# Two-MLP attention kernel: other PSUM banks for a pair's h, x forms of MLP 2 built during MLP 1's state rows, own buffers for the last evictions

## The chip, the cores and the metric

The kernel runs on one core of a Trainium2 chip. The metric is the device time of one execution in microseconds (us), the median of several. Work is spread over TensorE (PE; its weight loads are listed as PEld), VectorE (DVE), ScalarE (ACT) and the DMA queue that SyncE (SP) issues. Each engine runs its own list of instructions in order and waits on semaphores for the others.

## The reference

For 8 batch entries of 8 heads, 512 tokens and 32 states (D = 64), tokens attend to states and states attend to tokens; both results are laid side by side, so that there are 4608 rows of 512 numbers. Two MLPs with 2048 hidden units follow, the first with a squared ReLU, the second with an ELU:

```python
xread = softmax(scale * x @ state.T) @ state
sread = softmax(scale * state @ x.T) @ x
x = concat([xread, sread])              # rows of 512 = 8 heads x 64
x = relu(x @ w_in) ** 2 @ w_out         # MLP 1
h = x @ w_in2
out = where(h > 0, h, exp(min(h, 0)) - 1) @ w_out2   # MLP 2
```

## The kernel before, in words

Every product is made of three matmuls on operands that were split into a high part (an ACT copy) and a low part (a DVE subtraction); the helper `split` (L162) issues the two. Products of two token blocks at once use a seven-product scheme for 2x2 blocks, so they need sums of blocks ("forms") of x, of g and of the weights.

The work comes in this order. Batch entries 0 to 5 go one by one through MLP 1 (`block`, L477). Entries 6 and 7 go together (`pair`, L619): 32 tiles h (attention folded into m, `s1_x`), each read by a ReLU on ACT (L630), then `out_products` (L47) with its phases 1, 2, 6, 5, 7, 4, 3 of 48 matmuls into the accumulators x, y, z. Then come the 256 state rows of MLP 1 (L687 to L719): in turn i, PE makes h of slice i and adds slice i-2 to the four accumulators `acc`; ACT and DVE make the ReLU, its square, the split of that (gs) and the split of the next but one weight slice (`split_w1`, L449). Results of MLP 1 go through DRAM (`x2d`). MLP 2 reads them back (`load_xr`, L758), builds seven split forms of two entries (`x_forms`, L762: seven splits and four sums of 128x1024) and runs `first_product` and `second_product` for four such pairs, and last `state_block` (L884).

A scheduler orders each engine's list by its own model of time; pools decide which buffer or bank a tile gets. In the stage of the pair, PSUM has two banks for m (aux), and pools x, y, z of two banks in this order, which lie where `block` had its accumulators acc 0 and 1, acc 2 and 3, and its two h banks. The pair's h alternates between y and x (L624). In the state rows h lies on x, and acc on y and z; the weights v1 of the state rows (`load_v1`, L682) go into the 16 buffers gq1. MLP 2's own pools (L725 to L735) are opened after all of MLP 1's are closed. The last four evictions (L926) share three buffers `oo`.

Of the kernel before, what the change touches and what calls it, by code (L numbers as in the profile page):

```python
# [9 lines left out]
F32 = mybir.dt.float32  # L10
F32R = mybir.dt.float32r
# [3 lines left out]
ALU = mybir.AluOpType  # L15
AX = mybir.AxisListType

B, H, S, NS, D = 8, 8, 512, 32, 64
# [86 lines left out]
def attn_mlp_kernel(ctx: ExitStack, tc: tile.TileContext, xt, xn, st, w1, v1, w2, v2, outx, outs):  # L105
# [63 lines left out]
    if True:  # L169
# [270 lines left out]
        def operand_s():  # L440
            t = xc_p.tile([P, 2, KC, NST], F32R, name="sts", tag="xc")
            for k in range(2):
                split(t[:, HI, 2 * k:2 * k + 2], t[:, LO, 2 * k:2 * k + 2], stf[:, 2 * k:2 * k + 2])
            return t
# [163 lines left out]
        eu1_p = pool("eu1", 2)  # L608
        u21_p = pool("u21", 2)
        oo1_p = pool("oo1", 2)  # L610
        ps_x, ps_y, ps_z = [pool(n, 2, space=bass.MemoryType.PSUM) for n in ("psx1", "psy1", "psz1")]
        def weight1(j, f):
            t = wr1_p.tile([P, 2, 256], F32R, name="wr", tag="wr")
            src = {1: lambda: v1d[j][:, :, :256], 2: lambda: v1d[j + HF][:, :, :256],
# [4 lines left out]
        def pair(b0, bg):  # L619

            g = {q: [] for q in (11, 12, 21, 22)}
            for s in range(2 * FC):
                b, f = b0 + s // FC, s % FC
                ps = (ps_y, ps_x)[f % 2].tile([P, S], F32, name="h1", tag="yx"[f % 2])  # L624
                s1_x(b, ops[b], f, ps)
                t = g[(11, 12, 21, 22)[s // HF]]
                if f % 2 == 0:
                    t.append(gq1_p.tile([P, 2, S], F32, name="g1", tag="gq"))
                h = t[-1][:, f % 2]
                pace[:] = [nc.scalar.activation(out=h, in_=ps, func=AF.Relu)]  # L630
                if f % 2:
                    nc.vector.tensor_tensor(out=h, in0=h, in1=h, op=ALU.mult)
                else:
                    nc.scalar.activation(out=h, in_=h, func=AF.Square)
                if s >= 3 * HF and f % 2:
                    u = g[21][(f - HF) // 2]
                    nc.vector.tensor_tensor(out=u, in0=u, in1=t[-1], op=ALU.add)
                for todo in bg.get(s, ()):
                    todo()

            def step(n):
                for todo in bg.get(2 * FC + n, ()):
                    todo()

            def put(e, k, o):
                nc.sync.dma_start(out=x2d[b0 + e][:, k], in_=o)

            out_products(nc, split, g, weight1, 1, step, put, (gp1_p, eu1_p, u21_p, oo1_p), (ps_x, ps_y, ps_z))
# [28 lines left out]
            pair(b, bg)  # L677


        v1s = {}  # L680

        def load_v1(f):  # L682
            if f < FC:
                v1s[f] = gq1_p.tile([P, 2, DM], F32R, name="v1s", tag="gq")
                nc.sync.dma_start(out=v1s[f].bitcast(F32), in_=v1d[f])

        for f in range(4):  # L687
            load_v1(f)
        op = operand_s()
        gs = {}  # L690
        for i in range(FC + LAG):
            if i < FC:
                ps = ps_x.tile([P, NST], F32, name="h", tag="x")
                s1_s(op, i, ps)
                r = eu1_p.tile([P, NST], F32, name="r", tag="eu")
                nc.scalar.activation(out=r, in_=ps, func=AF.Relu)
                g = u21_p.tile([P, NST], F32, name="g", tag="u2")
                nc.vector.tensor_tensor(out=g, in0=r, in1=r, op=ALU.mult)
                t = gs[i] = gp1_p.tile([P, 2, NST], F32R, name="gs", tag="gp")
                split(t[:, HI], t[:, LO], g)  # L700
                if i + 2 < FC:
                    split_w1(i + 2)
                load_v1(i + 4)
            f = i - LAG
            if f < 0:
                continue
            if f == 0:
                acc = [p.tile([P, NST], F32, name="acc", tag=c) for p, c in ((ps_y, "y"), (ps_z, "z")) for _ in range(2)]
            w, t = v1s.pop(f), gs.pop(f)
            for k in range(KC):  # L710
                sl = slice(k * P, (k + 1) * P)
                mm3(acc[k], (w[:, HI, sl], w[:, LO, sl]), (t[:, HI], t[:, LO]), f == 0, f == FC - 1)
        for k in range(KC):
            o = oo1_p.tile([P, NST], F32, name="o", tag="o")
            if k % 2:
# [1 line left out]
            else:  # L717
                nc.scalar.activation(out=o, in_=acc[k], func=AF.Copy)
            nc.sync.dma_start(out=x2d[B][:, k], in_=o)  # L719
        double.close()  # L720
        one.close()


    pool2 = lambda name, bufs, **kw: ctx.enter_context(tc.tile_pool(name=name, bufs=bufs, reuse_waits="tile", **kw))
    xr_p = pool2("xr", 2)  # L725
    xf_p = pool2("xf", NF)
    wr_p = pool2("wr", 12)
    eu_p = pool2("eu", 5)
    u2_p = pool2("u2", 2)
    gq_p = pool2("gq", FC)  # L730
    gp_p = pool2("gp", 3)
    oo_p = pool2("oo", 3)
    ps_y = pool2("psy", 2, space=bass.MemoryType.PSUM)
    ps_z = pool2("psz", 3, space=bass.MemoryType.PSUM)
    ps_x = pool2("psx", 3, space=bass.MemoryType.PSUM)  # L735
    act, tt = nc.scalar.activation, nc.vector.tensor_tensor
    DM1, DM2 = slice(0, 2), slice(2, 4)

    def elu(h, out):

# [10 lines left out]
    def weight(name, j, f):  # L751
        t = wr_p.tile([P, 2, 256], F32R, name="wr", tag="wr")
        nc.sync.dma_start(out=t.bitcast(F32), in_=wf[name, j][:, f - 1])
        return t

    xf, xr = {}, {}

    def load_xr(b):  # L758
        xr[b] = xr_p.tile([P, KC, S], F32, name=f"xr{b}", tag="xr")
        nc.sync.dma_start(out=xr[b], in_=x2d[b])  # L760

    def x_forms(n):  # L762

        t1, t2 = xr[2 * n], xr[2 * n + 1]
        a11, a12, a21, a22 = t1[:, DM1], t1[:, DM2], t2[:, DM1], t2[:, DM2]

        def put(f, src):
            t = xf[n, f] = xf_p.tile([P, 2, 2, S], F32R, name=f"xf{n}_{f}", tag="xf")
            split(t[:, HI], t[:, LO], src)

        put(1, a11)
        yield
        put(2, a12)
        yield
        tt(out=a21, in0=a21, in1=a22, op=ALU.add)
        put(5, a21)
        yield
        tt(out=a11, in0=a21, in1=a11, op=ALU.subtract)
        put(6, a11)
        yield  # L780
        tt(out=a21, in0=a22, in1=a11, op=ALU.subtract)
        put(7, a21)
        yield
        put(4, a22)
        yield
        tt(out=a12, in0=a12, in1=a11, op=ALU.subtract)
        put(3, a12)
        yield

    def first_product(n, g):  # L790

# [92 lines left out]
    def state_block(prepared):  # L884
        for _ in prepared:
            pass
        nxt = iter(order[4:])
        ahead = iter(order[6:])

        def refill():  # L890
            x = next(nxt, None)
            if x:
                split_plain(*x)
            x = next(ahead, None)
            if x:
                load_plain(*x)

        gs, acc = {}, []
        for i in range(HF + 2):
            if i < HF:  # L900
                w = plain.pop(("w2", i))
                ps = ps_x.tile([P, 2, NST], F32, name="hs", tag="x")
                for r in range(2):
                    for d in range(2):
                        sl = [slice(r * 256 + k * P, r * 256 + (k + 1) * P) for k in range(2)]
                        product(nc, ps[:, r], [(w[:, HI, d, x], w[:, LO, d, x]) for x in sl],
                                [(xs[0][:, HI, 2 * d + k], xs[0][:, LO, 2 * d + k]) for k in range(2)],
                                r == 1 and d == 1, r == 0 and d == 0)
                g = gq_p.tile([P, 2, NST], F32, name="gsf", tag="gq")
                elu(ps, g)  # L910
                t = gs[i] = gq_p.tile([P, 2, 2, NST], F32R, name="gss", tag="gq")
                split(t[:, HI], t[:, LO], g)
                refill()
            j = i - 2
            if j < 0:
                continue
            if j == 0:
                acc = [p.tile([P, NST], F32, name="as", tag=c) for p, c in ((ps_y, "y"), (ps_z, "z")) for _ in range(2)]
            w, t = plain.pop(("v2", j)), gs.pop(j)
            for r in range(2):  # L920
                for m in range(KC):
                    sl = slice(m * P, (m + 1) * P)
                    product(nc, acc[m], [(w[:, HI, r, sl], w[:, LO, r, sl])], [(t[:, HI, r], t[:, LO, r])],
                            j == HF - 1 and r == 1, j == 0 and r == 0)
            refill()
        for m in range(KC):  # L926
            o = oo_p.tile([P, NST], F32, name="o", tag="o")
            if m % 2:
                nc.vector.tensor_copy(out=o, in_=acc[m])
            else:  # L930
                act(out=o, in_=acc[m], func=AF.Copy)
            nc.sync.dma_start(out=outs[m * P:(m + 1) * P, :], in_=o)

    for b in range(2):
        load_xr(b)
    for _ in x_forms(0):
        pass
    for n in range(B // 2):
        g = {}
# [51 lines left out]
```

## Time and profile before

| what | value |
|---|---|
| median of 3 runs | 1353.41 us (1352.47 to 1356.91) |
| span of the profiled execution, first to last instruction | 1350.5 us |
| its whole device time | not given by the page |
| PE busy | 1327.5 us, 98% of the span |
| PEld, DVE, ACT busy | 78%, 70%, 62% |
| granted TensorE clock, mean | 0.997 of full speed |

Busy shares are averages over the whole span. Where PE stands still is read from the list of waits and from the order of time; "idle before" in a row is the time in which the engine stood before that instruction, with what ended it.

### The profile page before, as it was taken

The page shows a single profiled execution, that of the slowest core. Times are in us where ns is not written, and L with a number is a line of the kernel's source. Part 1 is how long each engine was busy: PE and PEld are TensorE (multiplying, and loading weights), DVE is VectorE, ACT ScalarE, POOL GpSimd, SP SyncE. Part 2 cuts the span into 40 slices and gives each one's busy share as a digit, 9 for nine tenths or more (in the row PEclk, how much of TensorE's full clock was granted, in tenths as well). Part 3 has the DMA queues.
Part 4 walks back from the last instruction along what each step waited for, and adds up shares of the span by engine and source line. Part 5 has one row for each costly group of instructions (what it writes and reads, how often), then busy time and mean ns, then how long its engine had stood idle before and what let it go on. Part 6 is the DMA issues. An engine that isn't in the chain of part 4 may idle for free.

```text
span 1350.5 us, 19746 instructions
## 1 busy us (share of the span) xinstructions
PE 1327.5 (98%) x7064; PEld 1057.1 (78%) x7064; DVE 951.0 (70%) x1437; ACT 839.5 (62%) x1417; POOL 0.7 (0%) x6
## 2 busy tenths in 40 slices
PE   8989999999999999999999999999999999999998
PEld 6656777777777776778988888888888888888898
DVE  6997868686878865775576884579636884568644
ACT  5887758676777657644467843676446743666444
POOL 0000000000000000000000000000000000000000
PEclk9999999999999999999999999999999999999999
DMA  6988856575857424279077777767776777778732
GB/s 240 318 300 310 305 178 230 201 267 190 279 197 266 151 82 153 97 255 349 25 252 208 224 240 224 208 194 247 229 225 194 206 210 223 209 204 284 226 110 100
DMA packets 127729, 290.72 MB, mean 215 GB/s; under 512 B 13840, under 2 KB 22032, under 8 KB 124560
## 3 DMA queue, kind: packets, MB, share of 16 engines
q1 hardware_dynamic: 127632, 289.46, 66.3%
q8 instruction: 56, 0.92, 0.3%
q14 instruction: 41, 0.34, 0.1%
HBM read 212.86 MB, written 76.55 MB: 214 GB/s over the span
## 4 chain that ended last, share of the span: by engine, by line
PE 89%; DMA 5%; DVE 3%; ACT 3%; issue 1%; SPq 0%; ACTq 0%; DVEq 0%
PE x L43 16%; PE X L43 13%; PE z L43 8%; PE Z L43 6%; PE acc L158 6%; PE acc L159 6%; PE acc L160 6%; PE h L158 5%; PE h L159 4%; PE h L160 4%; PE y L43 4%; PE Y L43 3%; DMA raw_v<-in_v_dram 2%; PE mp L331 2%; PE hs L43 2%; PE as L43 2%
## 5 line engine op out<-in xcount | busy, mean ns | idle before, releaser
L163 ACT ACTIVATE gp<-g 128x1024 fp32r<-128x1024 f32 (+1 forms) x168 | 154.0, 917 | 146.0 <-PE x L43 69.5
L164 DVE TENSOR_TENSOR gp<-g,gp 128x1024 fp32r<-128x1024 f32 (+1 forms) x168 | 174.9, 1045 | 95.4 <-ACT gp L163 94.4
L43 PE MATMUL x<-gp,wr 128*128 128x512 f32 x960 | 223.5, 390 | 0.0
L43 PEld LDWEIGHTS x<-gp,wr 128*128 128x128 f32 x960 | 179.7, 188 | 39.4 <-ACT eu L71 1.9
L43 PE MATMUL X<-xf,wr 128*128 128x512 f32 x768 | 186.7, 390 | 0.0
L43 PEld LDWEIGHTS X<-xf,wr 128*128 128x128 f32 x768 | 143.4, 188 | 31.7 <-ACT u L748 1.3
L158 PE MATMUL acc<-gs,v 128*128 128x512 f32 x384 | 154.4, 402 | 3.8 <-DVE gs L474 1.9
L159 PE MATMUL acc<-gs,v 128*128 128x512 f32 x384 | 150.4, 392 | 0.0
L160 PE MATMUL acc<-gs,v 128*128 128x512 f32 x384 | 150.2, 392 | 0.0
L43 PE MATMUL z<-gp,wr 128*128 128x512 f32 x480 | 110.4, 389 | 0.0
L744 DVE SCALAR_TENSOR_TENSOR g<-r,g 128x512 f32<-128x512 f32 x96 | 63.9, 689 | 65.8 <-ACT r L743 65.8
L43 PEld LDWEIGHTS z<-gp,wr 128*128 128x128 f32 x480 | 90.1, 188 | 18.7
L158 PE MATMUL h<-at,m 128*128 128x512 f32 x256 | 103.0, 403 | 1.7 <-ACT r L469 1.7
L158 PEld LDWEIGHTS acc<-gs,v 128*128 128x128 f32 x384 | 72.0, 188 | 38.1 <-issue 15.9
L160 PE MATMUL h<-at,m 128*128 128x512 f32 x256 | 100.7, 395 | 0.5 <-ACT m L346 0.5
L159 PE MATMUL h<-at,m 128*128 128x512 f32 x256 | 101.0, 395 | 0.0
L43 PE MATMUL Z<-xf,wr 128*128 128x512 f32 x384 | 97.4, 389 | 0.0
L469 ACT ACTIVATE r<-h 128x512 f32<-128x512 f32 x96 | 57.1, 595 | 64.4 <-PE h L160 64.1
L742 ACT ACTIVATE r<-g 128x512 f32<-128x512 f32 x96 | 57.5, 625 | 57.5 <-DVE g L821 40.4
L160 PEld LDWEIGHTS acc<-gs,v 128*128 128x128 f32 x384 | 72.1, 188 | 19.8 <-issue 4.2
L159 PEld LDWEIGHTS acc<-gs,v 128*128 128x128 f32 x384 | 72.2, 188 | 18.6 <-issue 3.4
L43 PEld LDWEIGHTS Z<-xf,wr 128*128 128x128 f32 x384 | 72.1, 188 | 15.0
(145 smaller groups left out, 2173.6 us busy)
## 6 DMA issues: line engine op xcount, KB each, us to landing
wr<-f_v SPq DMA_DIRECT2D x256, 256.0 KB, 3.0
wr<-f_w SPq DMA_DIRECT2D x224, 256.0 KB, 2.9
f_v<-wf SPq DMA_DIRECT2D x40, 512.0 KB, 3.3
raw_w<-in_w_dram SPq DMA_DIRECT2D x32, 512.0 KB, 4.8
raw_v<-in_v_dram SPq DMA_DIRECT2D x32, 512.0 KB, 5.0
f_w<-wf SPq DMA_DIRECT2D x24, 512.0 KB, 2.8
xt<-in_xt_dram SPq DMA_DIRECT2D x8, 1024.0 KB, 6.9
xn<-in_xn_dram SPq DMA_DIRECT2D x8, 1024.0 KB, 6.1
```

Source lines behind the costliest of these rows:

```text
L43: nc.tensor.matmul(ps, wk[a], xk[b], start=start and k == 0 and i == 0, stop=last and k == len(w) - 1 and i == 2, skip_group_check=True)
L158: mm(ps, w[HI], x[LO], start=first, stop=False)
L159: mm(ps, w[HI], x[HI], start=False, stop=False)
L160: mm(ps, w[LO], x[HI], start=False, stop=last)
L163: copy = nc.scalar.activation(out=hi, in_=src, func=AF.Copy)
L164: nc.vector.tensor_tensor(out=lo, in0=src, in1=hi.bitcast(F32), op=ALU.subtract)
L331: mm(ps[e][32 * k:32 * k + 32, :], st_t[b][r, k, :], x(k, r), start=True, stop=True)
L469: pace[:] = [nc.scalar.activation(out=r, in_=ps, func=AF.Relu)]
L742: act(out=r, in_=h, func=AF.Relu, scale=-1.0)
L744: nc.vector.scalar_tensor_tensor(out=out, in0=r, scalar=-1.0, in1=h, op0=ALU.add, op1=ALU.max)
```

## The change

It does four things. The pools of the pair's stage are opened in the order y, x, z, and h alternates between z and y; h thus begins on `block`'s h banks and goes on with acc 0 and 1, and x is untouched until phase 1. The state rows get pools of their own (opened and closed again), and the buffers xr, wr and xf of MLP 2 are opened on SBUF's right side before the state rows; the weights v1 of the state rows use those wr buffers, in two halves, and the x forms of MLP 2's first pair are built in every second turn of the state rows. The last turn of `state_block` goes accumulator by accumulator, and its evictions use the five buffers eu.

```diff
-        ps_x, ps_y, ps_z = [pool(n, 2, space=bass.MemoryType.PSUM) for n in ("psx1", "psy1", "psz1")]
+        ps_y, ps_x, ps_z = [pool(n, 2, space=bass.MemoryType.PSUM) for n in ("psy1", "psx1", "psz1")]
...
-                ps = (ps_y, ps_x)[f % 2].tile([P, S], F32, name="h1", tag="yx"[f % 2])
+                ps = (ps_z, ps_y)[f % 2].tile([P, S], F32, name="h1", tag="zy"[f % 2])
...
+        double.close()
+        right = lambda name, bufs: ctx.enter_context(tc.tile_pool(name=name, bufs=bufs, side="right", reuse_waits="tile"))
+        xr_p = right("xr", 2)
+        wr_p = right("wr", 12)
+        xf_p = right("xf", NF)
+        rows = one.enter_context(ExitStack())
+        pool = pools(rows)
...
+        ps_y, ps_x, ps_z = [pool(n, 2, space=bass.MemoryType.PSUM) for n in ("psy2", "psx2", "psz2")]
...
         def load_v1(f):
             if f < FC:
-                v1s[f] = gq1_p.tile([P, 2, DM], F32R, name="v1s", tag="gq")
-                nc.sync.dma_start(out=v1s[f].bitcast(F32), in_=v1d[f])
+                v1s[f] = [wr_p.tile([P, 2, 256], F32R, name="v1s", tag="wr") for _ in range(2)]
+                for c, t in enumerate(v1s[f]):
+                    nc.sync.dma_start(out=t.bitcast(F32), in_=v1d[f][:, :, c * 256:(c + 1) * 256])
         for f in range(4):
             load_v1(f)
         op = operand_s()
+        for b in range(2):
+            load_xr(b)
+        forms = x_forms(0)
...
                 load_v1(i + 4)
+            if i > 1 and i % 2 == 0:
+                next(forms, None)
...
-            for r in range(2):
-                for m in range(KC):
+            last = j == HF - 1
+            for i in range(2 * KC):
+                r, m = (i % 2, i // 2) if last else divmod(i, KC)
...
-            o = oo_p.tile([P, NST], F32, name="o", tag="o")
+            o = eu_p.tile([P, NST], F32, name="o", tag="eu")
```

How the lists of instructions move, at the three places that the prediction speaks of. First PE's list from the last matmuls of entry 5 (acc) to the pair's first h (mp6_1 and mp6_2 are the products that become the next two slices of m). Before:

```order
L160 MATMUL acc_4501<-gs_5131,v1_15_1169 128x512
L331 MATMUL mp6_1_0_5272<-w1_10_322,st6_3872 32x512 [waits PE_49]
...
L331 MATMUL mp6_2_0_5326<-w1_20_489,st6_3872 32x512 [waits DVE_49]
L331 MATMUL mp6_2_1_5327<-w1_20_489,st6_3872 32x512 [waits DVE_49]
...
L158 MATMUL h1_5253<-at6_4710,m6_00_5017 128x512 [waits Activation_49]
```

and now:

```order
L160 MATMUL acc_4501<-gs_5131,v1_15_1169 128x512
L158 MATMUL h1_5253<-at6_4710,m6_00_5017 128x512
...
L331 MATMUL mp6_1_0_5272<-w1_10_322,st6_3872 32x512 [waits PE_49]
...
L158 MATMUL h1_5288<-at6_4710,m6_00_5017 128x512
...
L331 MATMUL mp6_2_0_5326<-w1_20_489,st6_3872 32x512 [waits DVE_49]
L331 MATMUL mp6_2_1_5327<-w1_20_489,st6_3872 32x512 [waits DVE_49]
L158 MATMUL h1_5263<-at6_4710,m6_00_5017 128x512 [waits Activation_49]
...
L158 MATMUL h1_5298<-at6_4710,m6_00_5017 128x512 [waits DVE_49]
...
L331 MATMUL mp6_3_0_5380<-w1_30_734,st6_3872 32x512 [waits DVE_49]
L158 MATMUL h1_5307<-at6_4710,m6_10_5282 128x512 [waits Activation_49]
```

Of the pair's first four h tiles one moved ahead of mp6_1, one between mp6_1 and mp6_2, and two ahead of mp6_2's last six rows; the first waits for nothing.

Second DVE's list. Before, the first sum of the x forms (xr1, which waits for its DMA) stood in the pair's product phases, between the splits gp of PE's operands:

```order
L164 TENSOR_TENSOR gp_5793<-g1_5403,gp_5793 128x512 [waits Activation_49]
L775 TENSOR_TENSOR xr1_7043<-xr1_7043 128x1024 [waits DMAHW1_49]
L164 TENSOR_TENSOR gp_5804<-g1_5403,gp_5804 128x512 [waits PE_49,Activation_49]
L164 TENSOR_TENSOR gp_5815<-g1_5422,gp_5815 128x512 [waits Activation_49]
```

Now no such row is there; at the end of the state rows (gs of slices 14 and 15) stands that of the next pair of entries, xr3:

```order
L164 TENSOR_TENSOR gs_6964<-g_6962,gs_6964 128x256 [waits Activation_49]
L751 TENSOR_TENSOR g_6999<-r_6997 128x256 [waits Activation_49]
L164 TENSOR_TENSOR gs_7001<-g_6999,gs_7001 128x256 [waits Activation_49]
L714 TENSOR_TENSOR xr3_7132<-xr3_7132 128x1024 [waits DMAHW3_49]
L751 TENSOR_TENSOR g_7035<-r_7033 128x256 [waits Activation_49]
L164 TENSOR_TENSOR gs_7037<-g_7035,gs_7037 128x256 [waits PE_49,Activation_49]
```

Before, the low half of one form of entries 0 and 1 stood among the rows of slice 15, and xr3 came later, in MLP 2.

Third SP's list now, from the pair's last stores to the state rows' first loads (before, all 16 v1 loads stood ahead of these stores):

```order
L647 DMA x2d6_129<-o_6350 128x512 [waits DMAHW7_49,DVE_49]
L735 DMA v1s_6392<-p_v10_1089 128x2x256 [waits DMAHW0_49,PE_49]
L735 DMA v1s_6393<-p_v10_1089 128x2x256 [waits DMAHW1_49]
...
L735 DMA v1s_6405<-p_v13_1411 128x2x256 [waits DMAHW7_49,PE_49]
L699 DMA xr0_6413<-x2d0_123 128x2048 [waits DMAHW0_49]
L699 DMA xr1_6415<-x2d1_124 128x2048 [waits DMAHW1_49]
L735 DMA v1s_6442<-p_v14_1511 128x2x256 [waits DMAHW2_49]
...
L735 DMA v1s_6892<-p_v115_1827 128x2x256 [waits DMAHW1_49]
L699 DMA xr2_7130<-x2d2_125 128x2048 [waits DMAHW2_49,DVE_49,Activation_49]
L699 DMA xr3_7132<-x2d3_126 128x2048 [waits DMAHW3_49,DVE_49,Activation_49]
L804 DMA wr_7139<-f_w20_2071 128x512 [waits DMAHW4_49,PE_49]
```

All 32 half loads of v1 now stand behind the stores, with xr0 and xr1 after the first eight; xr2 and xr3 stand ahead of MLP 2's first weights, and wait until the last forms have read xr0 and xr1.

## Rows read from the trace of the kernel before

**Rows 1.** The page: busy us of each engine (share of the span) x instructions.
```profile
PE 1327.5 (98%) x7064; PEld 1057.1 (78%) x7064; DVE 951.0 (70%) x1437; ACT 839.5 (62%) x1417; POOL 0.7 (0%) x6
```

**Rows 2.** Waits of PE, us in total, times, longest.
```profile
PE Y L43 <- DMA wr<-f_w: 1.8, 1, 1.8
PE y L43 <- DVE gp L164: 1.0, 1, 1.0
```

**Rows 3.** Timeline, block to pair: start, us, engine, line, operation, [idle before <- releaser].
```profile
504.62 0.39 PE L160 MATMUL acc<-gs,v 128*128 128x512 f32 x1
504.94 1.09 PE L331 MATMUL mp<-w,st 64*32 64x512 f32 x16
507.99 2.81 PE L331 MATMUL mp<-w,st 64*32 64x512 f32 x16 [1.96 <-DVE m L164]
510.73 0.79 PE L158 MATMUL h<-at,m 128*128 128x512 f32 x1
516.98 0.39 PE L158 MATMUL h<-at,m 128*128 128x512 f32 x1
```

**Rows 4.** Stretches of 1 us: length; busy of PE, PEld, DVE, ACT, POOL; granted clock; DMA share, GB/s.
```profile
510.00:511.00 1.00, 1.00 (x8) 0.27 (x2) 0.17 (x1) 0.00 (x0) 0.00 (x0) 0.50 0.84 311
512.00:513.00 1.00, 1.00 (x5) 0.79 (x5) 0.00 (x0) 0.00 (x0) 0.00 (x0) 0.92 0.51 183
690.00:691.00 1.00, 0.19 (x1) 0.22 (x2) 1.00 (x2) 1.00 (x2) 0.00 (x0) 1.00 1.06 398
```

**Rows 5.** Timeline and chain of waits, the pair's phase 2 (y).
```profile
572.56 4.24 PE L43 MATMUL y<-gp,wr 128*128 128x512 f32 x18
575.90 1.22 DVE L775 TENSOR_TENSOR xr<-xr 128x1024 f32<-128x1024 f32 x1 [2.65 <-DMA xr<-x2d]
585.00 10.88 PE x L43 x48
```

**Rows 6.** Timeline, state rows, begin and end.
```profile
639.78 1.00 SPq L646 DMA_DIRECT2D x2d<-o  x2
643.85 0.28 PE L158 MATMUL acc<-gs,v1s 128*128 128x256 f32 x1
674.34 0.41 DVE L164 TENSOR_TENSOR gs<-g,gs 128x256 fp32r<-128x256 f32 x1
684.53 0.39 PE L158 MATMUL acc<-gs,v1s 128*128 128x256 f32 x1 [0.20 <-DVE gs L164]
```

**Rows 7.** Loads: us to landing by group (page; then all DMA issues; then tiles wr before 560 us and xr).
```profile
wr<-f_v SPq DMA_DIRECT2D x256, 256.0 KB, 3.0
wr<-p_v SPq DMA_DIRECT2D x24, 256.0 KB, 5.3
DMA to landing us min/median/max: 4.2/5.4/5.8
DMA to landing us min/median/max: 4.8/5.8/8.0
```

**Rows 8.** The x forms' instructions (tile xf), ns min/median/max; state rows' and loads' stretches.
```profile
L163 ACT ACTIVATE xf<-xr x28: 1042/1055/1066, 681.8 to 1088.0; 128x1024 fp32r<-128x1024 f32 x28
L164 DVE TENSOR_TENSOR xf<-xr,xf x28: 1214/1218/1227, 682.9 to 1090.4; 128x1024 fp32r<-128x1024 f32 x28
639.30:686.00 46.70, 46.50 (x386) 46.24 (x385) 25.52 (x66) 22.92 (x64) 0.00 (x0) 1.00 0.17 58
637.00:639.00 2.00, 2.00 (x10) 1.65 (x10) 0.00 (x0) 0.00 (x0) 0.00 (x0) 1.00 1.02 414
```

**Rows 9.** Timeline and chain, the first matmuls of MLP 2.
```profile
686.07 1.55 PE L43 MATMUL Y<-xf,wr 128*128 128x512 f32 x6
702.14 4.08 PE X L43 x18
```

**Rows 10.** Timeline, the end of the program.
```profile
1337.39 8.80 PE L43 MATMUL as<-gss,pl 128*128 128x256 f32 x72
1347.39 0.42 DVE L929 COPY o<-as 128x256 f32<-128x256 f32 x1 [1.46 <-DMA out_dram<-o]
```

More of the change, by code (lines that the diff above doesn't have):

```diff
@@ L677, in attn_mlp_kernel, with load_xr, x_forms, put @@
             pair(b, bg)
+        double.close()
[5 more added lines that the diff above has]
+        pool = pools(rows)
+        gp1_p = pool("gp2", 4)
+        eu1_p = pool("eu2", 2)
+        u21_p = pool("u22", 2)
+        oo1_p = pool("oo2", 2)
+        ps_y, ps_x, ps_z = [pool(n, 2, space=bass.MemoryType.PSUM) for n in ("psy2", "psx2", "psz2")]
+        xf, xr = {}, {}
+        DM1, DM2 = slice(0, 2), slice(2, 4)
+        def load_xr(b):
+            xr[b] = xr_p.tile([P, KC, S], F32, name=f"xr{b}", tag="xr")
+            nc.sync.dma_start(out=xr[b], in_=x2d[b])
+        def x_forms(n):
+            t1, t2 = xr[2 * n], xr[2 * n + 1]
+            a11, a12, a21, a22 = t1[:, DM1], t1[:, DM2], t2[:, DM1], t2[:, DM2]
+            def put(f, src):
+                t = xf[n, f] = xf_p.tile([P, 2, 2, S], F32R, name=f"xf{n}_{f}", tag="xf")
+                split(t[:, HI], t[:, LO], src)
+            put(1, a11)
+            yield
+            put(2, a12)
+            yield
+            nc.vector.tensor_tensor(out=a21, in0=a21, in1=a22, op=ALU.add)
+            put(5, a21)
+            yield
+            nc.vector.tensor_tensor(out=a11, in0=a21, in1=a11, op=ALU.subtract)
+            put(6, a11)
+            yield
+            nc.vector.tensor_tensor(out=a21, in0=a22, in1=a11, op=ALU.subtract)
+            put(7, a21)
+            yield
+            put(4, a22)
+            yield
+            nc.vector.tensor_tensor(out=a12, in0=a12, in1=a11, op=ALU.subtract)
+            put(3, a12)
+            yield
         v1s = {}
@@ L710, in attn_mlp_kernel @@
             for k in range(KC):
-                sl = slice(k * P, (k + 1) * P)
-                mm3(acc[k], (w[:, HI, sl], w[:, LO, sl]), (t[:, HI], t[:, LO]), f == 0, f == FC - 1)
+                c, sl = k // 2, slice(k % 2 * P, (k % 2 + 1) * P)
+                mm3(acc[k], (w[c][:, HI, sl], w[c][:, LO, sl]), (t[:, HI], t[:, LO]), f == 0, f == FC - 1)
         for k in range(KC):
@@ L719, in attn_mlp_kernel @@
             nc.sync.dma_start(out=x2d[B][:, k], in_=o)
-        double.close()
+        rows.close()
         one.close()
[L724 to L735, printed above, removed]
+    pool = pools(ctx)
+    gq_p = pool("gq", FC)
+    eu_p = pool("eu", 5)
+    oo_p = pool("oo", 3)
+    u2_p = pool("u2", 2)
+    gp_p = pool("gp", 3)
+    ps_y = pool("psy", 2, space=bass.MemoryType.PSUM)
+    ps_z = pool("psz", 3, space=bass.MemoryType.PSUM)
+    ps_x = pool("psx", 3, space=bass.MemoryType.PSUM)
     act, tt = nc.scalar.activation, nc.vector.tensor_tensor
-    DM1, DM2 = slice(0, 2), slice(2, 4)
     def elu(h, out):
@@ L754, in weight @@
         return t
[L756 to L788, printed above, removed]
     def first_product(n, g):
@@ L919, in state_block @@
             w, t = plain.pop(("v2", j)), gs.pop(j)
-            for r in range(2):
-                for m in range(KC):
-                    sl = slice(m * P, (m + 1) * P)
-                    product(nc, acc[m], [(w[:, HI, r, sl], w[:, LO, r, sl])], [(t[:, HI, r], t[:, LO, r])],
-                            j == HF - 1 and r == 1, j == 0 and r == 0)
+            last = j == HF - 1
+            for i in range(2 * KC):
+                r, m = (i % 2, i // 2) if last else divmod(i, KC)
+                sl = slice(m * P, (m + 1) * P)
+                product(nc, acc[m], [(w[:, HI, r, sl], w[:, LO, r, sl])], [(t[:, HI, r], t[:, LO, r])],
+                        last and r == 1, j == 0 and r == 0)
             refill()
         for m in range(KC):
-            o = oo_p.tile([P, NST], F32, name="o", tag="o")
+            o = eu_p.tile([P, NST], F32, name="o", tag="eu")
             if m % 2:
@@ L932, in state_block @@
             nc.sync.dma_start(out=outs[m * P:(m + 1) * P, :], in_=o)
-    for b in range(2):
-        load_xr(b)
-    for _ in x_forms(0):
+    for _ in forms:
         pass
```

## The prediction

> **What bounds the kernel now.** I read the page first: PE is busy for 98% of the span [rows 1], so all its standing time together is some 23 us, and only what shortens that, the stretches at a lower clock or the end of the program can pay. The list of PE's waits comes next. Two of its entries lie where the change works: MLP 2's first weights, 1.8 us, and one wait of the pair's phase 2 for DVE, 1.0 us [rows 2]. The timeline adds two more: at the step from single entries to the pair PE stands for 1.96 us and then runs slowly [rows 3], and at the very end DVE's last copy waits 1.46 us for a buffer [rows 10]. The reader should see in these rows that each is a wait of a few us, once in the program. Nothing is repeated, so the change is worth the sum of its places and no more.
>
> The sum is made in the profiled execution, whose span is 1350.5 us. The median of the runs is 1353.4, 2.9 us more, which lies around the span; I carry the difference over to the median. About 0.3%, 4.1 us, is what a measurement of this kernel can tell from no change.
>
> **Part 1, h on other banks.** The last acc matmul starts at 504.62 and hands over at 504.85; the pair's fifth h starts at 516.98 [rows 3]. In these 12.1 us lie two sets of mp (1.09 each when PE runs freely) and four h of six matmuls. A matmul takes 10.88/48 = 0.227 us [rows 5], so the work is 2.2 + 5.4 = 7.6 us, and 4.5 us are lost: standing 1.96 before the second mp, a second mp of 2.81, and a first h begun at half clock [rows 3, 4]. Before, h needed the banks of acc 2 and 3, whose evictions stand on ACT and DVE behind the splits of m. Now the first h needs no wait, and one more h comes between the two mp sets. The split of the two halves of m takes about 2.0 us after mp6_1 ends (the 1.96 row) and mp6_1 ends 1.4 us later, behind the h; the second h covers 1.4 of these 2.0 us, so 0.6 to 0.8 us of standing stays. What is late next is the first row of mp6_3, which now stands right behind mp6_2: it waits for the same split once more, with nothing between, some 1.6 us, and the fifth h then waits for the first ReLU, which ACT's list has behind that split, 0.2 us. That is 2.5 us in place of 4.5: a gain of **2.0 us**. The bounds: 3.5 if mp6_3's row is hardly late, 0.5 if the clock falls as before. Phase 1 no longer shares x with h; from there it could gain at most 0.1, which I leave out.
>
> **Part 2, no x sum in the pair.** Phase 2 runs from 572.56 to 585.00, 12.44 us for 48 matmuls that take 10.88 in the next phase [rows 5]. In it DVE stands 2.65 us for the load of xr1, and the splits that PE needs queue behind it. The row is gone from there, so **1.55 us** go. The v1 loads leave this stage too; I cost that at nothing, since PE's list of waits has no load in it here.
>
> **Part 3, the state rows pay.** Three new waits.
> (a) The first v1 half is issued behind the pair's last two stores, which occupy SP from 639.78 to 640.78; PE wants it at 643.85 [rows 6]. A load of the same kind and size (wr from p_v, 1 KB runs) landed in 4.2 to 5.8 us, median 5.4, in a burst of twelve behind two stores [rows 7]. Near the low end of that burst, as the first of its queue, it takes 4.4: it lands at 645.2, **1.3 us** late. Bounds: 0 and 2.0. The Trainium skill (DMA: Bandwidth & Descriptors, Specifications) calls 512 B enough for line rate; by it a 1 KB run is as good as a 2 KB one. The rows speak against that: 2 KB runs take 3.0 [rows 7], so with that value the load lands at 643.8, this term is 0, and the sum below would be 4.6.
> (b) Seven splits and four sums of 128x1024 come between the small steps: 7 x 1.06 = 7.4 us on ACT, 11 x 1.22 = 13.4 us on DVE, where 25.5 of 46.7 us were busy and two low halves lay already [rows 8]. It fits in total. But two forms in a row hold ACT and DVE for 2.1 and 2.4 us, and the split of weight slice i has only the time from h of i-2 to h of i, three blocks of 1.44 us, for its own 1.5 to 2 us. At slices 7 and 8, where the first two forms stand, I count 0.3 and 0.6, together **0.9 us**. Bounds: 0 and 2.
> (c) The next sum, of xr3, stands in DVE's list before g and gs of slice 15, and its load is issued only when the last form has read xr0. The split of slice 12 ended at 674.75 [rows 6]; 2.2 us later by (a) and (b), plus 1.22 for that form and some queueing, gives 678.4 for the issue of xr2. A 1 MiB load takes at least 4.8 us [rows 7], and xr3 follows by 1.05 MB at 414 GB/s [rows 8], 2.5 us: it lands at 685.7. Then come the sum, 1.22, and g, gs high and gs low at 0.41 each, 2.6 us with handovers: 688.3. PE would want gs of slice 15 at 684.3 + 2.2 = 686.5, so it stands **1.8 us**. Bounds: 1 and 5. The engine that waits is DVE; behind the sum are two small steps that PE needs.
>
> **Part 4, the start of MLP 2.** From 686.07 to 702.14 lie 60 matmuls [rows 9], 13.6 us of work; 2.45 us are lost to the weights and the forms, and 0.2 to gs just before [rows 6]. Now the forms are there. The weights stand on SP behind xr2 and xr3, but DVE's wait in (c) gives them time: the seventh, which PE needs third, should land near 690, and PE asks for it two groups (2.7 us) after the last acc, past 692. So **2.65 us** go; if (c) is short, part of this comes back as a wait for weights, so the two are not independent.
>
> **Part 5, the end.** The last as matmul ends at 1337.39 + 8.80 = 1346.2; DVE's last copy starts at 1347.39 [rows 10] because its buffer still feeds a store. With five buffers it starts at 1346.25, and the store behind it moves with it: **1.15 us**. The other three accumulators finish earlier, which has no follower. I see no doubt above 0.3 us here.
>
> **The sum.** -2.0 - 1.55 + 1.3 + 0.9 + 1.8 - 2.65 - 1.15 = -3.35 us, 0.25%: a span of 1347.2, a median of **1350.1 us**. The rest of the program, from the first products of MLP 2 to the last turn, has the same order on every engine, and I cost it at nothing.
>
> **The rivals.**
> - *The state rows hide it all* (chance 0.38). If v1 lands in time, (a) is 0, and the forms cost 0.3 in place of 0.9. For it: DMA engines are idle once the stores are out (17% busy in that stage before [rows 8]). Against: no load with 1 KB runs landed in 3.0 us. Sum -3.35 - 1.3 - 0.6 = -5.25: 1348.2.
> - *The pair's begin keeps its loss* (chance 0.10). The ReLUs of the first h stand on ACT behind the splits of m, so the new order may only trade one wait for another: part 1 gives nothing. Sum -1.35: 1352.1.
> - *DVE's wait for xr3 decides* (chance 0.08), the other side. The longest 1 MiB load took 8.0 [rows 7]; with 2.5 behind it xr3 lands at 688.9, PE stands 5.0 in place of 1.8, and the clock falls. It did so at the pair's begin: after thin mp matmuls and standing, 0.50 of full speed, that is 1.2 GHz, until 512.1 [rows 4], some 3.2 us, 1.6 lost. After the 1.8 us without weights at 690.8 it stayed at 2.4 GHz [rows 4]. The Trainium skill (TensorE: Matmul & The Clock Gate, Part 1) has the clock throttled when idle and released by activity; both rows agree with that, and neither says on which side a wait of 3 to 5 us falls. Sum -3.35 + 3.2 + 1.6 = +1.45: 1354.9. It turns to slower than before when PE stands over 3.5 us there and the clock falls, so when xr3 lands after 687.4.
>
> **How the numbers follow.** The forecast (0.44) is the sum; its own range is 1349.3 to 1351.5. Faster by over 0.3% is the first rival, 0.38. Slower by over 0.3% is the worse half of the third, with a little for a mishap, 0.05. The rest is 0.57. The range runs from 1347.4, a little below the first rival, to 1353.4, past the second; outside lie most of the third and the first rival's best cases.
>
> **What would show it.** In the profile after: four h tiles before mp6_3, and the fifth h about 2 us sooner after the last acc; no wait for DVE in phase 2; a wait of acc for v1s at the first acc; small waits of h for w1s near slices 7 and 8; DVE idle for the xr load and PE for gs of slice 15; no wait of Y for weights; the last copy right after the last matmul. I am wrong if PE does not stand at slice 15, if the first v1 costs nothing, or if the waits in the state rows sum to over 6 us.

## The result, and the profile after

The change makes the kernel slower: 1360.49 us (median of 8, 1358.76 to 1364.78) against 1353.47 (median of 8), a ratio of 1.0056 with a 95% interval of 1.0041 to 1.0070. The forecast was 1350.1. The profiled execution after is the slowest of its eight (1364.78), with a span of 1363.0 us, 12.5 more than before. The medians are 7.0 us apart, so some 5 us of the 12.5 belong to the two profiled executions and not to the change.

First the span cut into stages, each from the start of one matmul to the start of another, as the timeline gives them. Two later versions stand beside (r5 and r6, below). Times are in us; "to" means up to the start of the matmul named.

| stage | before | after | r5 | r6 |
|---|---|---|---|---|
| begin to the last acc of entry 5 | 504.62 | 507.12 | 506.14 | 507.15 |
| to the pair's phase 1 | 56.98 | 58.55 | 58.57 | 57.03 |
| the pair's phases | 77.94 | 76.49 | 76.48 | 76.49 |
| state rows of MLP 1, first h to first Y | 46.53 | 50.34 | 47.94 | 47.20 |
| first 42 matmuls of MLP 2 | 11.82 | 9.66 | 9.67 | 9.69 |
| the rest of MLP 2's token rows | 579.79 | 589.01 | 579.94 | 579.91 |
| state rows of MLP 2 to the last as | 68.23 | 68.40 | 67.67 | 67.67 |
| last as to the end | 4.57 | 3.40 | 3.40 | 3.40 |

The first line is not laid to the change: PE's list is the same up to there, and in the profiled executions of this study that stage ends between 504.01 and 507.17 us in kernels made from the one before, between 505.32 and 508.55 in those made from the one after. The line that decides is the sixth: 9.2 us in a stage in which PE's list is the same in both kernels. The groups of TensorE show it, of the kernel after (line, engine, operation; busy us, mean ns of one; idle before):

```profile
L43 PE MATMUL x<-gp,wr 128*128 128x512 f32 x960 | 228.9, 395 | 0.0
L43 PE MATMUL X<-xf,wr 128*128 128x512 f32 x768 | 186.6, 390 | 0.0
L43 PE MATMUL z<-gp,wr 128*128 128x512 f32 x480 | 113.3, 395 | 0.0
```

and of the kernel before:

```profile
L43 PE MATMUL x<-gp,wr 128*128 128x512 f32 x960 | 223.5, 390 | 0.0
L43 PE MATMUL X<-xf,wr 128*128 128x512 f32 x768 | 186.7, 390 | 0.0
L159 PE MATMUL h<-at,m 128*128 128x512 f32 x256 | 101.0, 395 | 0.0
L43 PE MATMUL z<-gp,wr 128*128 128x512 f32 x480 | 110.4, 389 | 0.0
```

The first product (X) is as fast as ever; the second (x, z) has a longer mean, with no idle time before it. (One group of the kernel before, h<-at,m, had that longer mean of 395 already.) The chain of waits tells the spacing (start, length, engine, tile, line, number of matmuls); after, the pair's phase in MLP 1, a piece of the first product, and two phases of the second:

```profile
576.72 10.88 PE y L43 x48
706.41 4.08 PE X L43 x18
780.42 11.25 PE y L43 x48
791.67 11.24 PE x L43 x48
```

and before:

```profile
775.82 10.88 PE y L43 x48
786.70 10.88 PE x L43 x48
```

So 48 matmuls take 11.24 us, 234 ns each, where they took 10.88, 227 each. It is not the clock, which was granted in full there (the third number from the end of the row, 1.00):

```profile
780.50:791.00 10.50, 10.50 (x46) 8.47 (x45) 10.11 (x10) 5.64 (x6) 0.00 (x0) 1.00 0.70 198
```

The second loss is in the state rows of MLP 1. PE's waits there, two rows of DVE and the first Y, in order of time:

```profile
647.59 0.36 PE L158 MATMUL acc<-gs,v1s 128*128 128x256 f32 x1 [0.95 <-DVE g L751]
649.25 0.38 PE L158 MATMUL acc<-gs,v1s 128*128 128x256 f32 x1 [0.59 <-DMA v1s<-p_v]
661.81 0.39 PE L158 MATMUL h<-sts,w1s 128*128 128x256 f32 x1 [0.18 <-ACT w1s L163]
662.69 0.38 PE L158 MATMUL h<-sts,w1s 128*128 128x256 f32 x1 [0.38 <-ACT w1s L163]
688.39 1.22 DVE L714 TENSOR_TENSOR xr<-xr 128x1024 f32<-128x1024 f32 x1 [1.00 <-DMA xr<-x2d]
690.44 0.42 DVE L164 TENSOR_TENSOR gs<-g,gs 128x256 fp32r<-128x256 f32 x1 [0.48 <-ACT gs L163]
692.51 1.55 PE L43 MATMUL Y<-xf,wr 128*128 128x512 f32 x6
```

There are two waits for the first two halves of v1 (the first is put down to DVE, but it goes when only the loads are moved: r6), two small ones for w1s, and none for gs of slice 15 although DVE stood for xr3. Behind the two waits the clock was granted at 0.50, 1.2 GHz, and then in full again; the same happened behind the pair's begin:

```profile
520.00:523.00 3.00, 3.00 (x8) 2.30 (x7) 0.69 (x1) 2.10 (x5) 0.00 (x0) 0.50 1.03 341
649.60:652.60 3.00, 3.00 (x16) 3.00 (x15) 0.00 (x0) 0.00 (x0) 0.00 (x0) 0.50 0.88 280
653.00:654.00 1.00, 1.00 (x11) 1.00 (x10) 0.47 (x2) 0.89 (x3) 0.00 (x0) 1.00 1.02 360
```

The pair's begin after, to be held against [rows 3]:

```profile
507.12 0.39 PE L160 MATMUL acc<-gs,v 128*128 128x512 f32 x1
508.82 1.09 PE L331 MATMUL mp<-w,st 64*32 64x512 f32 x16
511.42 1.60 PE L331 MATMUL mp<-w,st 64*32 64x512 f32 x4
515.90 1.07 PE L331 MATMUL mp<-w,st 64*32 64x512 f32 x12
518.42 1.04 PE L331 MATMUL mp<-w,st 64*32 64x512 f32 x2 [1.45 <-DVE m L164]
519.39 0.50 PE L158 MATMUL h<-at,m 128*128 128x512 f32 x1
```

And the end, against [rows 10]: the last copy now starts as the last matmul ends.

```profile
1351.25 8.61 PE L43 MATMUL as<-gss,pl 128*128 128x256 f32 x72
1359.90 0.42 DVE L947 COPY o<-as 128x256 f32<-128x256 f32 x1 [0.98 <-PE as L43]
```

### The profile page after: what moved, and what is told of

Its sections match the earlier page's. It is cut to its first block, busy times and chain, and to the rows that moved or that the text cites. A ratio compares the mean times of both kernels' runs of the same rounds, so it can differ in the third digit from the quotient of the medians.

```text
span 1363.0 us, 19764 instructions
## 1 busy us (share of the span) xinstructions
PE 1339.0 (98%) x7064; PEld 1058.1 (78%) x7064; DVE 951.3 (70%) x1437; ACT 839.6 (62%) x1417; POOL 0.7 (0%) x6
## 4 chain that ended last, share of the span: by engine, by line
PE 91%; DMA 3%; DVE 3%; ACT 2%; issue 1%; SPq 0%; ACTq 0%; DVEq 0%
PE x L43 16%; PE X L43 13%; PE z L43 8%; PE acc L158 7%; PE Z L43 6%; PE acc L160 6%; PE acc L159 6%; PE h L158 5%; PE h L160 4%; PE h L159 4%; PE y L43 4%; PE Y L43 3%; PE mp L331 3%; PE hs L43 2%; PE as L43 2%; DMA raw_w<-in_w_dram 1%
## 5 line engine op out<-in xcount | busy, mean ns | idle before, releaser
L43 PE MATMUL x<-gp,wr 128*128 128x512 f32 x960 | 228.9, 395 | 0.0
L43 PE MATMUL z<-gp,wr 128*128 128x512 f32 x480 | 113.3, 395 | 0.0
```

Source lines behind the costliest of these rows:

```text
L43: nc.tensor.matmul(ps, wk[a], xk[b], start=start and k == 0 and i == 0, stop=last and k == len(w) - 1 and i == 2, skip_group_check=True)
```

## The experiments

**What slows the second product.** The change moved gp (the moving operand) and wr (the weights) to other places of a partition. "Place" below is the byte at which a tile begins in each partition, as the compiled program has it, and "distance" the place of the moving operand less that of the weights, modulo 256. Before, xf, wr and gp all lay at 128 modulo 256; after, wr and xf lie at 224 and gp at 128. In MLP 1 the pair's gp and wr lie alike in both kernels.

*r1_right32*: the changed kernel with

```diff
+        right("pad", 1).tile([P, 8], F32, name="pad")
         xr_p = right("xr", 2)
```

> The changed kernel with one empty tile of 32 bytes ahead of xr on SBUF's right side, so that xr, wr and xf begin at multiples of 64 bytes per partition (in the changed kernel they lie 32 bytes off, while gp lies at a multiple of 64). Theory A (a matmul runs slower when its weights and its moving operand lie at different places within 64 bytes): a phase of 48 matmuls of MLP 2's second product takes 10.88 us again in place of 11.24, 28 phases x 0.36 = 10.1 us come back: ratio to the kernel before about 0.998. Theory B (what counts is that gp and wr changed sides of SBUF): the phase stays 11.24, ratio about 1.0055. Theory C (traffic of the other engines or DMAs into the new buffers slows the reads): stays 11.24, as B.

Measured: ratio 1.0046 (1.0034 to 1.0059); the phase takes 11.20 us. All places are multiples of 64 now, and it stays slow: theory A falls.

*r2_gp32*: the changed kernel with

```diff
+    pool("pad", 1).tile([P, 8], F32, name="pad")
     gp_p = pool("gp", 3)
```

> The changed kernel with one empty tile of 32 bytes ahead of gp, so that gp lies 32 bytes off a multiple of 64, as wr does. Theory A: the second product's phases take 10.88, ratio about 0.998. Theory A2 (it is the weights' own place that counts, 32 bytes off): phases stay 11.24, ratio about 1.0055. Theories B and C: 11.24.

Measured: 1.0041 (1.0027 to 1.0054), matmuls 233.3 ns apart. A said fast and falls again. A2 said slow, but r1 had the weights at a multiple of 64 and was slow too. That leaves B and C, or another rule of distance.

*r3_before_wr32*: the kernel before with

```diff
+    pool2("pad", 1).tile([P, 8], F32, name="pad")
     wr_p = pool2("wr", 12)
+    pool2("pad2", 1).tile([P, 8], F32, name="pad2")
```

> The kernel before with 32 empty bytes on either side of MLP 2's wr: wr lies 32 bytes off, xf and gp at multiples of 64, sides and order as before. Theory A: both products of MLP 2 slow down, the second by 28 x 0.36 = 10.1 us and the first, 1344 matmuls in four pairs, by 1344 x 7.5 ns = 10.1 us too: ratio about 1.015, six matmuls X 1.40 us in place of 1.36. Theories B and C: nothing changes, ratio 1.000.

Measured: 1.0125 (1.0111 to 1.0139). Sides, order and traffic are as before, and both products are slow; in the chain of waits:

```profile
703.28 4.20 PE X L43 x18
707.48 1.40 PE Y L43 x6
778.90 11.20 PE y L43 x48
```

against 4.08 for 18 matmuls X before [rows 9]. So neither B (sides) nor C (traffic) is needed for the loss: 32 bytes between the two operands are enough. Whether they add to it, the next run tells.

*r5_gp_match*: the changed kernel with gp at wr's place, and no instruction moved:

```diff
+    pool("pad", 1).tile([P, 472], F32, name="pad")
     gp_p = pool("gp", 3)
```

> The changed kernel with 1888 empty bytes ahead of gp, so that gp and wr begin at the same place within 2048 bytes of a partition (2016); no instruction moves. Theory D (a 512-column matmul takes 226.7 ns where its weights and its moving operand begin at the same place within 512 or 2048 bytes, and 230 to 234 ns where not; so far all rows fit: xf and wr alike and fast in both kernels, gp and wr alike before and not alike now, not alike either with 32 bytes added on one side): a phase takes 10.88 us, ratio 0.998. Theory B (sides of SBUF): 11.24, ratio 1.0055.

Measured: 0.9992 (0.9983 to 1.0000), and the phases are back:

```profile
776.72 10.88 PE y L43 x48
787.60 10.88 PE x L43 x48
```

This one edit takes back all of the stage but 0.15 us (579.94 in the table), and the ratio falls by 0.0064, 8.7 us. The cause is shown: 1888 empty bytes undo the loss, with wr still on the right side of SBUF and no instruction moved.

*s1_scan*: the kernel before, where each tile gp begins at a place shifted by its phase, and xf by its pair:

```diff
-                t = gp_p.tile([P, 2, unit, S], F32R, name="gp", tag="gp")
+                n = 2 * unit * S
+                t = gp_p.tile([P, n + (256 if unit == 2 else 0)], F32R, name="gp", tag="gp")
+                o = shift[f] if unit == 2 else 0
+                t = t[:, o:o + n].rearrange("p (a u s) -> p a u s", a=2, u=unit)
```

> The kernel before with wider buffers gp and xf (place of wr within 512 bytes kept, 128), in which the tile begins at a shifted place: in the 28 phases of the second products gp is shifted by 0, 32, 64, ... 480 bytes, then 4, 8, 16, 48, 512, 1024, 272, 240, 256, 64, 192, 0; in the four first products xf by 0, 128, 256, 512. Theory D with a period of 512 bytes: only the shifts 0, 512 and 1024 take 226.7 ns a matmul, all others 230 to 235. With a smaller period (64 or 128 bytes) its multiples are fast too. If only theory B holds, all are 226.7.

One execution, 1364.76 us. Phases at shifts of 32, 64, 96; then 256; 512; 272, 240, 256, 64 (of each phase the row of the chain):

```profile
780.04 11.20 PE y L45 x48
791.25 11.00 PE x L45 x48
802.25 11.21 PE z L45 x48
...
936.64 10.90 PE y L45 x48
...
1147.54 10.91 PE z L45 x48
...
1245.66 11.12 PE y L45 x48
1256.77 11.36 PE x L45 x48
1268.13 10.91 PE z L45 x48
1279.04 11.00 PE x L45 x48
```

The mean from start to start of matmuls that follow each other without a wait: 227.0 to 227.3 ns at shifts of 0, 256, 512 and 1024, 229.1 or 229.2 at 64 and 320, and 231.5 to 236.6 at all others (32, 96, 128, 160, 192, 224, 288, 352 to 480, and also 4, 8, 16, 48, 240, 272). For xf: 227.2, 232.5, 227.0, 227.0 at 0, 128, 256, 512. The period is 256 bytes, not 512 or 64. The earlier runs fit: after, distance 160, 234.2 ns (scan 234.2); r1 and r2, distance 192 at different places, 233.3 in both (scan 233.2 to 233.5); h<-at,m of MLP 1, distance 64 in both kernels, 229.6 (scan 229.1). One group does not: acc<-gs,v of MLP 1, at distance 0 in both kernels, takes 228.3. Why the distance counts, no run shows.

*s2_scan256*: matmuls of 256 columns, in the kernel before:

```diff
-        t = xf_p.tile([P, 2, 2, 512], F32R, name="pl", tag="xf")
+        t = xf_p.tile([P, 4 * S + 512], F32R, name="pl", tag="xf")
+        t = t[:, 8 * j:8 * j + 4 * S].rearrange("p (a u s) -> p a u s", a=2, u=2)
```

> The kernel before; in the last stage (state rows of MLP 2, matmuls of 256 columns) the weight tiles pl begin at places shifted by 32 bytes times the slice, 0 to 224, so that hs and as run at eight different distances between moving operand and weights within 256 bytes. In the runs so far these matmuls took 120.0 ns at equal places, 118 to 119.5 at three others and 114.4 at the one where weights lie 64 bytes behind the moving operand's place (distance 192). If the distance alone decides here too, the eight slices show these values again, 114.4 at the shift of 64, none below 113, and 120.0 at the shift of 0. If not, all are 120.

One execution, 1355.38 us. Measured for as, shifts 0 to 224 in steps of 32: 119.8, 118.4, 114.1, 117.5, 119.0, 119.5, 117.9, 117.8 ns. Right for as; for hs wrong, which takes 117.9 at 64 and no less than 116.8 anywhere. With 256 columns equal places are among the slowest, not the fastest (as 119.8; hs 119.7, and 119.8 at a shift of 160). The state rows of MLP 1 agree in later runs: at distance 192, h<-sts,w1s takes 115.6 ns in r9 and 117.6 in r8 (120.0 before, at 0), and acc<-gs,v1s 115.6 in r12 (118.5 after, at 224). Why, no run tells.

**What the change does apart from that.** *r4_before_banks*: part 1 alone (the two lines on PSUM pools and h of the diff above) in the kernel before.

> The kernel before with part 1 of the change alone: the pair's h on other PSUM banks. The prediction's step: from the last acc matmul of entry 5 to the pair's phase 1 57.1 us before, 55.1 now, ratio 0.9985. What the changed kernel's trace says: 58.7, since the standing moves behind mp6_2 and the clock falls there, at 519.8, with full h work behind it: ratio 1.001.

Measured: 1.0008 (0.9999 to 1.0017), the stretch 57.01 with the clock up, so neither 55.1 nor 58.7. There is no gain, and a loss is not beyond the interval.

*r6_wr_early*: r5 with wr opened behind xf on the right side, so that the first v1 halves stand ahead of the pair's last two stores.

```diff
-        wr_p = right("wr", 12)
         xf_p = right("xf", NF)
+        wr_p = right("wr", 12)
```

> The same with wr opened last on the right side: it then lies over buffers gq1 that come free before the pair's last stores, and the first v1 halves are issued ahead of the last two of these stores. If the wait for the first v1 halves and the lower clock behind it are what the state rows lost, their stretch (first h to first Y, 50.35 us in the changed kernel, 46.53 before) comes to 46.7 to 47.7 us and the ratio to 0.9955. If the forms' splits on ACT and DVE are what they lost, the stretch stays above 49 and the ratio at 0.998.

Measured: 0.9983 (0.9974 to 0.9993), state rows 47.20 as the first theory had it. The ratio is 0.0028 above the 0.9955 of that theory: r5 had already come out 0.0012 above the 0.998 expected of it, and with state rows of 47.94 in its profiled execution it left less to gain. The waits for v1 and w1s are gone; what is left stands in one row of PE's waits, and the longer of the two waits is slice 15, behind DVE's wait for xr3:

```profile
PE acc L158 <- DVE gs L164: 0.9, 2, 0.6
683.82 1.23 DVE L714 TENSOR_TENSOR xr<-xr 128x1024 f32<-128x1024 f32 x1 [1.90 <-DMA xr<-x2d]
686.34 0.39 PE L158 MATMUL acc<-gs,v1s 128*128 128x256 f32 x1 [0.57 <-DVE gs L164]
```

So the loads and the clock were most of the loss, not the forms' splits: moving the loads takes back 3.1 of 3.8 us, and the waits for w1s go with it. *r7_banks_back*: the same with h on the banks of before.

> The same as the last with the pair's h on the banks of before (part 1 taken back). If part 1 loses 1.6 us, as the stretch from the last acc of entry 5 to phase 1 says (57.1 before, 58.7 in the changed kernel), the ratio falls by 0.001 to 0.9943 and the stretch is 57.1 again. If that loss is noise of one run: the same ratio as the last run.

Measured: 0.9976 (0.9965 to 0.9986), stretch 56.69 with the clock down in it, as before. The two ratios do not tell the banks apart.

**A version that beats both.** *r8_placed* and *r9_before_placed* put further operands at the distances that the scans favour. r8 is r6 with empty tiles around xc (the pool of at) and ahead of gp2, gq and gp; r9 is the kernel before with empty tiles around xc and around gq. Both have

```diff
+    pool("pad", 1).tile([P, 48], F32, name="pad")
     xc_p = pool("xc", 2)
+    pool("pad", 1).tile([P, 16], F32, name="pad")
     sf_p = pool("sf", 1)
```

> The changed kernel with wr opened last and every pair of operands placed by what the scans say; no instruction moves against r6_wr_early: gp and wr at equal places; 192 empty bytes ahead of xc, so that at and m of MLP 1 stand at equal places within 256 bytes (64 apart in all kernels so far: 229.7 ns); gs of the state rows 192 away from v1s, gss 192 away from pl. Theory D with a period of 256 bytes: h<-at,m 226.8 ns (768 matmuls, -2.2 us), acc<-gs,v1s and as<-gss,pl 114.2 ns in place of 119.5 and 118 (-1.0 and -0.7 us), together some -4 us: ratio 0.995. If the scans hold only for MLP 2's own stage: as r6_wr_early, 0.998.

> The kernel before with the same idea and nothing else: 192 empty bytes ahead of xc, 64 behind it, 192 ahead of gq and 64 behind it. Theory D: h<-at,m 226.8 ns in place of 229.6 (-2.2 us), as 114.2 in place of 120 (-1.1 us): ratio 0.9975, no wait changes. Else 1.000.

Measured: 0.9974 (0.9964 to 0.9983) and 0.9981 (0.9973 to 0.9990). The 256-column part came (as 113.8 or 113.9 ns in both), the part of MLP 1 did not: h only went to 229.2 (r8) or 229.0 ns (r9), acc<-gs,v rose from 228.3 to 229.2 or 229.3, and an entry took 74.35 us in place of 74.18 (from one row sc to the next). Moving at puts it away from the place of v and gs. *r11_before_m* moves m instead:

```diff
+    pool("pad", 1).tile([P, 16], F32, name="pad")
     m_p = pool("m", 4)
+    pool("pad", 1).tile([P, 48], F32, name="pad")
     xa_p = pool("xa", 1)
```

> The kernel before with 64 empty bytes ahead of m and 192 behind it, nothing else: in MLP 1 the weights m, the moving operand at, the weights v and the moving operand gs then all begin at the same place within 256 bytes (m alone stood 64 off). Theory E (what counts is the place of the weights that are loaded while a matmul streams, so the next matmul's weights too, against that matmul's moving operand): h<-at,m 226.8 ns in place of 229.6 and acc<-gs,v 226.9 in place of 228.3, 768 x 2.8 + 1152 x 1.4 = 3.8 us, ratio 0.9972. Theory D alone (only a matmul's own two operands): h 226.8, acc stays 228.3, 2.2 us, ratio 0.9984.

Measured: 0.9997 (0.9987 to 1.0007). h goes to 227.6 ns, acc stays at 228.4: so h is as theory D has it, and E falls on the second count. D alone does not cover MLP 1 either: in r9 only at had moved there, and acc, whose own two operands kept their equal places, became slower. What else counts is open. An entry takes 74.00 us, 0.18 less (the two rows sc below), of which eight entries make 1.4 us; the ratio neither shows nor excludes it.

```profile
137.48 1.02 PE sc L333 x16
211.48 1.02 PE sc L333 x16
```

*r12_all_placed* is r6 with m, gp2, gq and gp placed, *r13_placed_banks* the same with h on the banks of before.

> The changed kernel with wr opened last, gp and wr alike, m moved as in the run beside it, gs of the state rows and gss 192 away from their weights. Theory E: as r6_wr_early (0.9983) less 3.8 us in MLP 1, 1.0 in the state rows and 0.7 at the end: ratio 0.9943. Theory D alone: 0.9955.

> The last version with the pair's h on the banks of before (part 1 taken back). In the profiled runs so far the stretch from the last acc of entry 5 to phase 1 is 56.4 to 57.0 us with the banks of before, and with the others 57.0 where the clock stays up and 58.4 to 58.6 where it falls. If that is part 1's doing: stretch 56.4 to 57.0, ratio 0.9965 in place of 0.9974. If it is the run's and not the banks': 58.4 can occur here too, same ratio.

Measured: 0.9974 (0.9962 to 0.9986), short of both expectations, with the clock down at the pair's begin (stretch 58.35); and 0.9963 (0.9950 to 0.9977), stretch 56.79. Why r12 falls short, no run shows. The last has the lowest ratio here, 1348.46 us, but the interval holds both of its expectations, so r12 and r13 are not told apart. Part 1's new banks are left with no gain in any run; that they cost something is likely from the stretches (58.35 to 58.57 in four profiled executions and 57.0 in four, against 56.4 to 57.0 in the eight with the banks of before), but no ratio shows it.

## Why the prediction was wrong

**The rest of the program.** The step that failed is the last sentence of the sum: that the rest "has the same order on every engine, and I cost it at nothing". The order is indeed the same; the places of gp and wr are not, and 9.2 of the 12.5 us of span lie there; r5 takes them back. No rival held this case. The diff showed that both pools move, and the trace of before held the warning: h<-at,m and z<-gp,wr have the same shape, yet means of 395 and 389 ns and spacings of 229.6 and 226.7.

**Part 1** (-2.0): +1.6 in the profile. The step that failed is "2.5 us in place of 4.5". From the last acc to the fifth h are 519.39 - 507.12 = 12.27 us, before 12.36 [rows 3]. The first four rows of mp6_2 took 1.5 us (each stands in the list with a wait of its own for DVE's split), and mp6_3's rows came with 1.45 us of standing and 1.0 us of their own; 4.4 us are lost again. Then the clock fell at 519.8, over full-width h. In r6 the same wait of 1.45 stands, the clock stayed up, and the stretch is 57.03: no gain and no loss, as the second rival had it. With the clock down over h, which that rival did not have, it became a loss.

**Part 2** (-1.55): -1.45. Right.

**Part 3** (+4.0): +3.8, right as a sum by luck and wrong inside. (a) 1.3 was expected; the first acc came 1.1 late, and the second half, which I had not counted, another 0.7. The third rival had a falling clock, at slice 15; it fell here instead. r5, with the same list, had neither the second wait nor the lower clock and needed 2.4 us less, which leaves some 1.7 for the clock. (b) 0.9: the two rows for w1s sum to 0.56 and split one block, 0.8 in all (starts of 661.81 and 662.69 against those that even spacing gives), at slice 7 as said. Some of it came back, as acc<-gs,v1s took a median of 117 ns in place of 120. (c) 1.8: none, which the prediction itself had named as a sign of being wrong. xr3 came to DVE at 688.39, which is the 685.7 of the prediction plus the 2.6 by which the state rows began later; but PE came later still, held up by (a) and its clock. Where those go (r6), slice 15 waits 0.57.

The loads of v1 did land late, with a median of 5.7 us where 5.3 stood in [rows 7]. That their 1 KB runs are the reason, as (a) took it, is not shown: the loads of wr that follow have 2 KB runs and took 5.4 in the same stretch.

```profile
v1s<-p_v SPq DMA_DIRECT2D x32, 256.0 KB, 5.7
wr<-f_w SPq DMA_DIRECT2D x7, 256.0 KB, 5.4
```

**Part 4** (-2.65 with the gs wait): -2.16 in the first 42 matmuls, and no wait of Y for weights is left. **Part 5** (-1.15): -1.17.

With the places mended (r5), the change gives 0.9992 (0.9983 to 1.0000), about 1.1 us, where 3.35 were forecast. In r5's profiled execution part 1 is 3.6 us short of its forecast (+1.6 for -2.0), and part 3 is 2.6 better (+1.4 for +4.0).

## What to carry to other kernels

A change of pools or sides moves operands, and in the second product here a 512-column matmul cost 1% more at a distance of 64 bytes between its operands, modulo 256, and 2 to 4% more at every other distance tried but 0: after such a change, compare the spacing of matmuls that wait for nothing, group by group, before looking for waits. An empty tile ahead of one operand mended it (1888 bytes in r5). And a wait in TensorE's list costs its length plus what the clock does behind it, which differed from run to run for the same wait.

## What was not expected of the hardware

Spacing by distance, at full clock, as read above: 512 columns (second product) 226.7 to 227.3 ns at 0, 229.1 at 64, 231.5 to 236.6 at the others tried; 256 columns (as) 119.8 at 0, 114.1 at 192. The Trainium skill (SBUF — State Buffer, Who interferes with whom) gives TensorE two read ports of its own, one for the moving operand and one for the weights, and calls them independent. No run here measures the ports. But the two streams are not independent of each other's place: r3 is slow with sides, order and traffic as before, and 32 bytes between the operands. The same page of the Trainium skill (SBUF — State Buffer, Operand start alignment) asks only for a multiple of the element size and says that this is about legality, not speed; here 4 bytes of shift cost 236.3 against 227 ns.

The clock's fall is not a matter of the wait alone: after 1.45 us of standing behind thin mp matmuls it was 0.50 of full speed in r5 and 1.00 in r6, with the same rows ahead of it:

```profile
519.40:521.40 2.00, 2.00 (x6) 1.61 (x5) 0.69 (x1) 1.23 (x3) 0.00 (x0) 0.50 0.97 321
```

```profile
519.40:521.40 2.00, 2.00 (x10) 1.63 (x10) 1.17 (x2) 2.00 (x5) 0.00 (x0) 1.00 1.10 365
```

Ten matmuls fit into the same two microseconds in place of six.
